# First stage of a banded-attention and gated-product kernel: 256 moving columns read as two halves of 128 in alternation

## The chip, the cores and the metric

The kernel runs on one core of a Trainium2 chip. Its time is the device time in microseconds (us). Before the change the median of three runs is 746.01 us (744.32, 746.01, 748.61). The engines are named as in the profile: PE is TensorE's matmul side, PEld its weight loads, DVE is VectorE, ACT is ScalarE, POOL is GpSimd, SP is SyncE, which issues all DMAs here.

## The reference

Attention over 8 batches and 8 heads, with a band of 32 positions to either side plus 32 global keys, and 32 global queries that see everything, is followed by two products that gate each other and two more products:

```python
x = attn_out.transpose(0, 2, 1, 3).reshape(4352, 512)   # 8 batches x (32 global + 512 local) rows
a = x @ w1                    # w1, w2: 512 x 1024
b = x @ w2
h = (a * b) @ w3              # w3: 1024 x 1024
return h @ w_out              # w_out: 1024 x 512
```

All is float32. Nothing stands between `@ w3` and `@ w_out`, so the kernel multiplies these two weights together once (`fold`, into W34, 1024 x 512) and computes `(a * b) @ W34`.

## The kernel before, in words

The whole program is one static order of steps (the table `ORDER_OF`), interleaved over all engines. What matters here are two stages of TensorE.

**First stage** (`first`, lines 548 to 550 before). The rows of x come in blocks of 256 tokens, 16 blocks of local tokens (`key[0] < B`: batch and half of the batch) and one of the 256 global tokens. For a block, x lies transposed in SBUF: four tiles of 128 features, each `[128, 2, 256]`, with a high part `x[:, 0]` and a low part `x[:, 1]` in the type float32r, which together carry float32. Weights w1 and w2 are split alike into `wh` and `wl`. For each of 8 groups of 128 hidden columns (`m`), for w1 and w2 (`c`, PSUM tiles `ap` and `bp`), and for each of the 4 feature tiles there are three matmuls: wh by high (L548), wh by low (L549), wl by high (L550). The weights, 128 x 128, are the stationary operand and are loaded anew for each matmul (PEld), x's 256 columns are the moving one. That makes 8 x 2 x 4 x 3 = 192 matmuls a block, 3072 over the 16 local blocks and 192 for the global one (tiles `xg`).

**Between the stages**, for two groups `m` at a time: one copy of `ap` to SBUF (`gate_a`, on DVE or ACT), the product with `bp` (`gate_b`, L558, DVE), its high part (`gate_hi`, L442 of a helper) and its low part (`gate_lo`, L445), both float32r tiles `gh` and `gl` of `[128, 2, 256]`. `ap` and `bp` have one buffer each, so the next pair's matmuls wait for `gate_a` and `gate_lo`.

**Second stage** (`second`, L578 to L580). Here gh and gl are stationary, 128 tokens at a time, and a row of 512 columns of W34 is moving; it accumulates in PSUM tiles `acc` of 128 tokens x 512. W34 lies in SBUF with its even columns in front and its odd columns behind them (`by_halves`, `in_pairs`), and the matmul reads it back in order, in alternation from two halves that lie 256 elements apart:

```python
wh, wl = (w.rearrange("p (a c) -> p c a", a=2) for w in W34[m])
```

After 8 groups each `acc` is copied to SBUF (`evict`, L585) and stored (`store`, L593): 128 rows of the output, 2 KB each, 256 KB a DMA, 32 of them for local tokens.

Ahead of and among these stages run the weights' unpacking and folding (L605 to L609, L695 with plain float32 operands), transposes on TensorE (L388), scores (L350, L473) and values (L402, L502) of the attention, as many small matmuls of 32 columns by 64 or 128 rows.

Of the kernel before, what the change touches and what calls it, by code (L numbers as in the profile page):

```python
# [18 lines left out]
def i(ap):  # L19
# [161 lines left out]
    out="D726 A732 D872 D875 A999 A1006 D1109 A1130 A1241 D1254 A1376 D1380 A1519 A1530 D1656 D1666 D1791 D1803  "  # L181
# [20 lines left out]
def band_attention_glu_kernel(  # L202
# [14 lines left out]
    nc = tc.nc  # L217
    B, NP = q_t.shape[0], q_t.shape[1] // 2
    NM, NU = B * NP, B * NP // 2
    TG = 32 * B  # L220
    S = 544
# [317 lines left out]
    def first(key, w, m, c):  # L539

        k_s = f"{key[0]}_{key[1]}_{m - m % 2}"
        if m % 2 == 0:
            T["ab", c] = ps_1.tile([128, 2, 256], F32, tag="ab"[c], name="ab"[c] + "p" + k_s)
        wh, wl = W12[m]
        d = T["ab", c][:, m % 2, 0:w]
        for k in range(4):
            x = X[key[0], k, key[1]]
            nc.tensor.matmul(d, wh[:, k, c, :], x[:, 0, 0:w], start=(k == m % 2 == 0), stop=False, skip_group_check=True)  # L548
            nc.tensor.matmul(d, wh[:, k, c, :], x[:, 1, 0:w], start=False, stop=False, skip_group_check=True)  # L549
            nc.tensor.matmul(d, wl[:, k, c, :], x[:, 0, 0:w], start=False, stop=(k == 3), skip_group_check=True)  # L550

    def gate_a(w, q, eng):
        T["a", q % 2] = p1.tile([128, 2, 256], F32, tag=("as", "g")[q % 2], name="as_")
# [34 lines left out]
    def store(key, w, t):  # L588
        tw = min(w, 128)
        o = T.pop(("o", key, t))  # L590
        if key[0] < B:
            r = key[0] * S + 32 + 256 * key[1] + t
            nc.sync.dma_start(out[r : r + 128], o)  # L593
        else:
            nc.sync.dma_start(out.rearrange("(b s) c -> b s c", s=S)[t // 32 : (t + tw) // 32, 0:32], o[0:tw])

# [274 lines left out]
    def quarter(k, q):  # L871
# [8 lines left out]
        for s, tag in enumerate("ab"):  # L880
            take(tag, 1, (tag, n), ("first", k, m, s))
            for j in range(2):
                me = ("first", k, m + j, s)
                add(me, "PE", ready + made(m + j) + [("first", k, m, s)] * j, first, key, w, m + j, s)
                read(me, (tag, n), *xs)
# [24 lines left out]
        if q == 3:  # L910
            for e in range(0, w, 128):
                me = ("out", k, e)
                take("o", NO, ("o", k, e), me)
                add(me, "ACT DVE", [("second", k, 7, (e,) if last else None)], evict, key, w, e)
                read(me, ("acc", k, e))
                add(("store", k, e), "SP", [me], store, key, w, e)
                read(("store", k, e), ("o", k, e))
# [79 lines left out]
    with tc.manual_schedule(engines=None):  # L997
        for _, n, e in in_order(steps, after):
            fn, args, choice = emit[n]
            k = steps[n][0]  # L1000
# [66 lines left out]
```

## Time and profile before

| what | before |
|---|---|
| median of 3 runs | 746.01 us |
| profiled execution | 744.0 us, its span 742.2 us |
| PE busy | 724.9 us (98%) |
| PEld busy | 645.6 us (87%) |
| DVE / ACT / POOL busy | 429.2 / 292.0 / 115.0 us |
| granted TensorE clock, mean | 0.995 |
| first-stage matmuls on local tokens | 3072 |

Busy time of PE is a poor measure, since matmuls overlap in the pipeline: one of the first stage lasts about 277 ns from its start to its end, while they start some 113 ns apart. The chain of waits shows what each one adds to the end; it gives each matmul the time until the next one starts.

### The profile page before, as it was taken

The page shows a single profiled execution, that of the slowest core. Times are in us where ns is not written, and L with a number is a line of the kernel's source. Part 1 is how long each engine was busy: PE and PEld are TensorE (multiplying, and loading weights), DVE is VectorE, ACT ScalarE, POOL GpSimd, SP SyncE. Part 2 cuts the span into 40 slices and gives each one's busy share as a digit, 9 for nine tenths or more (in the row PEclk, how much of TensorE's full clock was granted, in tenths as well). Part 3 has the DMA queues.
Part 4 walks back from the last instruction along what each step waited for, and adds up shares of the span by engine and source line. Part 5 has one row for each costly group of instructions (what it writes and reads, how often), then busy time and mean ns, then how long its engine had stood idle before and what let it go on. Part 6 is the DMA issues. An engine that isn't in the chain of part 4 may idle for free.

```text
span 742.2 us, 24082 instructions
## 1 busy us (share of the span) xinstructions
PE 724.9 (98%) x10036; PEld 645.6 (87%) x10036; DVE 429.2 (58%) x1275; ACT 292.0 (39%) x853; POOL 115.0 (15%) x165
## 2 busy tenths in 40 slices
PE   4899999999999999999999999999999999999998
PEld 3345598989999998999999999999999999999997
DVE  2788898766565475554765557655566635432232
ACT  3678887654243324324244333244423241301010
POOL 2044565300020002130110001101020110000000
PEclk9899999999999999999999999999999999999999
DMA  8998567797576755577767396756575965520010
GB/s 246 293 303 265 165 216 227 204 265 190 160 214 177 197 152 184 168 191 196 231 174 216 110 243 192 229 137 180 160 216 165 243 169 130 143 72 15 1 43 29
DMA packets 96500, 131.98 MB, mean 178 GB/s; under 512 B 15592, under 2 KB 57704, under 8 KB 96392
## 3 DMA queue, kind: packets, MB, share of 16 engines
q1 hardware_dynamic: 96392, 130.45, 62.1%
q8 instruction: 79, 1.29, 0.7%
q14 instruction: 29, 0.24, 0.1%
HBM read 92.65 MB, written 37.75 MB: 176 GB/s over the span
## 4 chain that ended last, share of the span: by engine, by line
PE 90%; DMA 6%; DVE 1%; POOL 1%; issue 1%; ACT 0%; SPq 0%; DVEq 0%; POOLq 0%
PE ap L548 8%; PE acc L578 8%; PE bp L548 8%; PE ap L549 8%; PE ap L550 8%; PE bp L550 8%; PE bp L549 8%; PE acc L580 8%; PE acc L579 8%; PE w L695 5%; PE v L402 4%; PE s L350 4%; DMA raw_wo<-in_wo_t_dram 3%; PE sg L473 2%; PE gx L502 2%; DMA raw_w12s<-in_w_t_dram 1%
## 5 line engine op out<-in xcount | busy, mean ns | idle before, releaser
L548 PE MATMUL ap<-x,w12h 128*128 128x256 f32 x512 | 143.9, 281 | 0.0
L548 PE MATMUL bp<-x,w12h 128*128 128x256 f32 x512 | 143.8, 281 | 0.0
L549 PE MATMUL ap<-x,w12h 128*128 128x256 f32 x512 | 141.9, 277 | 0.0
L549 PE MATMUL bp<-x,w12h 128*128 128x256 f32 x512 | 141.8, 277 | 0.0
L550 PE MATMUL ap<-x,w12l 128*128 128x256 f32 x512 | 141.8, 277 | 0.0
L550 PE MATMUL bp<-x,w12l 128*128 128x256 f32 x512 | 141.8, 277 | 0.0
L362 ACT ACTIVATE P<-P,mn 128x128 f32<-128x128 f32 x256 | 100.4, 394 | 58.3 <-DVE mn L357 27.1
L548 PEld LDWEIGHTS bp<-x,w12h 128*128 128x128 f32 x512 | 96.3, 188 | 3.3 <-issue 1.6
L548 PEld LDWEIGHTS ap<-x,w12h 128*128 128x128 f32 x512 | 96.3, 188 | 3.2 <-issue 1.8
L549 PEld LDWEIGHTS bp<-x,w12h 128*128 128x128 f32 x512 | 96.2, 188 | 1.4 <-issue 0.2
L549 PEld LDWEIGHTS ap<-x,w12h 128*128 128x128 f32 x512 | 96.2, 188 | 0.9
L550 PEld LDWEIGHTS bp<-x,w12l 128*128 128x128 f32 x512 | 96.2, 188 | 0.0
L550 PEld LDWEIGHTS ap<-x,w12l 128*128 128x128 f32 x512 | 96.1, 188 | 0.0
L357 DVE CUSTOM_DVE_ANT_0 P<-s,cs 128x128 f32<-128x128 f32 x256 | 62.4, 281 | 33.5 <-PE s L350 30.4
L695 PE MATMUL w<-wo,w3f 128*128 128x512 f32 x128 | 61.4, 620 | 4.7 <-DVE w3f L609 4.7
L326 POOL COPY K<-K 128x480 f32<-128x480 f32 x24 | 15.6, 656 | 242.3 <-DMA K<-in_kp_t_dram 204.4
L695 PEld LDWEIGHTS w<-wo,w3f 128*128 128x128 f32 x128 | 23.6, 196 | 30.8 <-issue 22.9
L362 ACT ACTIVATION_READ_ACCUMULATOR P<-P,mn 128x1 f32 x256 | 48.4, 189 | 0.0
L316 POOL COPY V<-vg 32x1024 f32<-32x1024 f32 x26 | 27.0, 1045 | 76.2 <-PE gx L507 44.2
L370 DVE STREAM_TRANSPOSE P<-P 128x1024 f32<-128x1024 f32 x28 | 34.7, 1238 | 5.7 <-ACT P L362 5.6
L316 ACT COPY V<-vg 32x1024 f32<-32x1024 f32 x31 | 32.4, 1045 | 14.0 <-PE gx L507 13.4
L350 PE MATMUL s<-K,q 64*32 64x128 f32 x2048 | 37.6, 277 | 0.0
(786 smaller groups left out, 1362.4 us busy)
## 6 DMA issues: line engine op xcount, KB each, us to landing
Pd<-P SPq DMA_DIRECT2D x112, 128.0 KB, 2.7
Pt<-Pd SPq DMA_DIRECT2D x28, 512.0 KB, 3.9
raw_w<-in_w_t_dram SPq DMA_DIRECT2D x24, 512.0 KB, 5.7
V<-in_v_t_dram SPq DMA_DIRECT2D x56, 192.0 KB, 5.0
K<-in_kp_t_dram SPq DMA_DIRECT2D x36, 272.0 KB, 3.8
V<-in_v_t_dram SPq DMA_DIRECT2D x36, 256.0 KB, 4.9
out_dram<-o SPq DMA_DIRECT2D x34, 256.0 KB, 3.8
q<-in_q_t_dram SPq DMA_DIRECT2D x32, 256.0 KB, 4.5
```

The costliest lines, as they stand in the source:

```text
L316: (nc.scalar.copy if eng is nc.scalar else eng.tensor_copy)(to, src)
L350: nc.tensor.matmul(block(st[:, h], x, 128 * g), q[64 * h : 64 * h + 64, c : c + 32], window(m, h, 4 * g + x), start=True, stop=True, skip_ ...
L357: nc.vector.tensor_tensor_reduce(T["P", m][:, :, h, g], chunks(T["s", m][:, h, 128 * g : 128 * g + 128]), chunks(masks[g]), -0.125, 3.0e38 ...
L362: nc.scalar.activation(P, P, AF.Exp, bias=T["mn", m][:, g, h : h + 1], scale=-1.0, accum_out=T["sm", m][:, g, h : h + 1])
L370: nc.vector.transpose(P, P)
L548: nc.tensor.matmul(d, wh[:, k, c, :], x[:, 0, 0:w], start=(k == m % 2 == 0), stop=False, skip_group_check=True)
L549: nc.tensor.matmul(d, wh[:, k, c, :], x[:, 1, 0:w], start=False, stop=False, skip_group_check=True)
L550: nc.tensor.matmul(d, wl[:, k, c, :], x[:, 0, 0:w], start=False, stop=(k == 3), skip_group_check=True)
L578: nc.tensor.matmul(a, gh[:, m % 2, sl], wh, start=(m == 0), stop=False)
L579: nc.tensor.matmul(a, gh[:, m % 2, sl], wl, start=False, stop=False)
L580: nc.tensor.matmul(a, gl[:, m % 2, sl], wh, start=False, stop=(m == 7))
L695: nc.tensor.matmul(T["w34", t], T["w3f", t, j // 4][:, j % 4], T["wo"][:, j], start=(j == 0), stop=(j == 7))
```

## The change

The moving operand of the first stage is the same 256 columns in another order: column 0 of the block, column 128, 1, 129, and so on (for the global block `a=1`, which leaves the order as it was). The results in `ap`, `bp`, `gh`, `gl` and `acc` then hold the tokens in that order, and the store of 128 rows writes 64 pairs of rows, the two of a pair 128 rows apart. No instruction is added, removed or moved on any engine; after the change the two stage lines are numbered one higher for the first stage (L549 to L551) and the second stage is L579 to L581.

```diff
         for k in range(4):
             x = X[key[0], k, key[1]]
-            nc.tensor.matmul(d, wh[:, k, c, :], x[:, 0, 0:w], start=(k == m % 2 == 0), stop=False, skip_group_check=True)
-            nc.tensor.matmul(d, wh[:, k, c, :], x[:, 1, 0:w], start=False, stop=False, skip_group_check=True)
-            nc.tensor.matmul(d, wl[:, k, c, :], x[:, 0, 0:w], start=False, stop=(k == 3), skip_group_check=True)
+            hi, lo = (x[:, e, 0:w].rearrange("p (a b) -> p b a", a=2 if key[0] < B else 1) for e in range(2))
+            nc.tensor.matmul(d, wh[:, k, c, :], hi, start=(k == m % 2 == 0), stop=False, skip_group_check=True)
+            nc.tensor.matmul(d, wh[:, k, c, :], lo, start=False, stop=False, skip_group_check=True)
+            nc.tensor.matmul(d, wl[:, k, c, :], hi, start=False, stop=(k == 3), skip_group_check=True)
...
         if key[0] < B:
-            r = key[0] * S + 32 + 256 * key[1] + t
-            nc.sync.dma_start(out[r : r + 128], o)
+            r = key[0] * S + 32 + 256 * key[1]
+            to = out[r : r + 256].rearrange("(a b) c -> b a c", a=2)[t // 2 : t // 2 + 64]
+            nc.sync.dma_start(to, o)
```

## Rows read from the trace of the kernel before

**Rows 1.** The page: span, and the granted clock in 40 slices of it.
```profile
span 742.2 us, 24082 instructions
...
PEclk9899999999999999999999999999999999999999
```

**Rows 2.** The page: the chain that ended last, shares of the span by engine.
```profile
PE 90%; DMA 6%; DVE 1%; POOL 1%; issue 1%; ACT 0%; SPq 0%; DVEq 0%; POOLq 0%
```

**Rows 3.** Waits of PE: waiting line, releaser, us in total, times, longest.
```profile
PE w L695 <- DVE w3f L609: 4.7, 1, 4.7
PE v L402 <- DVE raw_w12s L605: 0.2, 1, 0.2
```

**Rows 4.** The page's groups: first stage, output ap (bp alike); busy us, mean ns.
```profile
L548 PE MATMUL ap<-x,w12h 128*128 128x256 f32 x512 | 143.9, 281 | 0.0
...
L549 PE MATMUL ap<-x,w12h 128*128 128x256 f32 x512 | 141.9, 277 | 0.0
```

**Rows 5.** The chain in order of time, first stage: start us, us, what.
```profile
300.20 0.11 PE ap L548
...
302.92 1.03 PE v L402 x64
```

**Rows 6.** The same chain, a run of the second stage.
```profile
313.08 0.22 PE acc L578
...
315.67 0.12 PE bp L548
```

**Rows 7.** Instructions of line 548: duration ns min/median/max, first and last start.
```profile
L548 PE MATMUL ap<-x,w12h x512: 276/276/388, 96.6 to 730.3; 128*128 128x256 f32 x171
```

**Rows 8.** Instructions of line 579, the second stage: one stationary tile.
```profile
L579 PEld LDWEIGHTS acc<-w34l,gh__1203 x4: 188/189/189, 107.4 to 109.4; 128*128 128x128 f32 x4
L579 PE MATMUL acc<-w34l,gh__1203 x4: 379/379/379, 107.7 to 109.6; 128*128 128x512 f32 x4
```

**Rows 9.** Line 548 at 404.2 us: the first matmul after second-stage ones.
```profile
L548 PEld LDWEIGHTS ap<-x,w12h x1: 189/189/189, 404.0 to 404.0; 128*128 128x128 f32 x1
L548 PE MATMUL ap<-x,w12h x1: 286/286/286, 404.2 to 404.2; 128*128 128x256 f32 x1
```

**Rows 10.** Line 578 at 401.5 us: weights loaded while no full matmul streams.
```profile
L578 PEld LDWEIGHTS acc<-w34h,gh__6050 x1: 186/186/186, 401.5 to 401.5; 128*128 128x128 f32 x1
L578 PE MATMUL acc<-w34h,gh__6050 x1: 483/483/483, 401.5 to 401.5; 128*128 128x512 f32 x1
```

**Rows 11.** Timeline at 401.5 us: start us, us, engine, line, operation.
```profile
401.54 0.19 PEld L578 LDWEIGHTS acc<-w34h,gh__6050 128*128 128x128 f32 x1
...
401.65 0.19 PEld L579 LDWEIGHTS acc<-w34l,gh__6050 128*128 128x128 f32 x1
```

**Rows 12.** Line 695, all of it.
```profile
L695 PE MATMUL w<-wo,w3f x128: 592/592/1221, 15.2 to 94.8; 128*128 128x512 f32 x128
```

**Rows 13.** Line 695 at 55.3 us, right behind four transposes.
```profile
L695 PEld LDWEIGHTS w<-wo,w3f x2: 190/191/192, 55.2 to 55.3; 128*128 128x128 f32 x2
L695 PE MATMUL w<-wo,w3f x1: 595/595/595, 55.3 to 55.3; 128*128 128x512 f32 x1
```

**Rows 14.** The chain in order of time: these four transposes.
```profile
54.99 0.44 PE t L388 x4
```

**Rows 15.** Timeline at 640 us: bp's last reader and its next writer.
```profile
639.23 0.65 DVE L445 TENSOR_TENSOR gl__9759<-bp,gh__9757 128x512 fp32r<-128x512 f32 x1
...
640.09 0.30 PE L548 MATMUL bp<-x,w12h 128*128 128x256 f32 x1
```

**Rows 16.** Waits of all engines: DVE for the first stage.
```profile
DVE bp L558 <- PE bp L550: 134.3, 47, 6.2
```

**Rows 17.** Page, DMA issues: KB each, median us to landing.
```profile
Pd<-P SPq DMA_DIRECT2D x112, 128.0 KB, 2.7
...
out_dram<-o SPq DMA_DIRECT2D x34, 256.0 KB, 3.8
```

**Rows 18.** Timeline: the end of the program.
```profile
738.77 0.59 ACT L585 COPY o<-acc 128x512 f32<-128x512 f32 x1 [17.31 <-PE acc L580]
```

## The prediction

> **What bounds the kernel now.** I read the page first, then the chain of waits, then single instructions of the two TensorE stages, to the nanosecond, since the change touches only how long one of 3072 matmuls takes.
>
> The chain says that PE is the bound: 90% of the span lies on it [rows 2], and after the weights are folded (95 us) PE has hardly a wait: its whole list is one of 4.7 us early on, 0.2 us once, and the warm-up's [rows 3]. [...] So a nanosecond off each first-stage matmul comes off the span, as long as no wait replaces it.
>
> A busy time says nothing of a pipelined matmul, so I use two measures. Pace: how far apart starts are. From 300.20 to 302.92 us there are 24 first-stage matmuls [rows 5], 2720 / 24 = 113.3 ns each. From 313.08 to 315.67 there are 12 of the second stage [rows 6], 2590 / 12 = 215.8 ns. Duration: 276 ns at the least and in the median for the first stage [rows 7], 379 for the second [rows 8]. 276 - 113 and 379 - 216 are both 163, so pace = duration - 163, and either can be read for the other.
>
> What is 113.3 made of? [...] 256 columns would be 106.7 + 2.5 = 109.2, a duration of 272. The first stage is 4 ns over this at its best and 5 in the mean: L549 has a mean of 277 [rows 4]. Two causes can make that.
>
> (a) The stream. Right behind a second-stage matmul, a first-stage matmul has had its weights for 100 ns: their load began at 404.0 and took 189, the matmul began at 404.2. Nothing but its own columns can hold it up, and yet it takes 286 [rows 9], 14 over 272. In the second stage, which reads 512 columns in alternation from two halves, there is no such excess: minimum, median and maximum are all 379 [rows 8]. The chip thus reads these float32r columns one behind the other slower than in alternation; beside the weight load the excess varies, and it settles at 4 in long runs.
>
> (b) The weight load. Each first-stage matmul has a load of 128 columns, which can start only when the matmul before begins to stream. Where no full matmul streams, a load takes 186 and its matmul waits 483 - 379 = 104 ns for it [rows 10]; the next load starts 0.11 after the first [rows 11], as soon as that matmul streams. A cycle of load and handing over is thus between 104 and 110; I take 108.5, just below 109.2. But beside a streaming matmul loads take longer: 188 to 189 in the second stage [rows 8], 190 to 192 beside transposes, where the matmul behind them lasts 595 instead of 592 [rows 12, 13], so that it starts to stream 3 ns late. The transposes' pace is 440 / 4 = 110 [rows 14], near 109.2, so they are a fair model; 109.2 + 3 = 112.2.
>
> **The change part by part.** *The moving operand.* 3072 matmuls read in alternation; instruction count, weights and order are the same. The stream should fall from a pace of 114 (277 - 163) to 109.2; the load then decides. Its bounds: 109.2 if loads take no longer than alone, 112.2 if they behave as beside transposes, 113.3 if today's pace is already the load's. The nearest rows are the loads beside an alternating stream, 188.5, 2.5 over the lone load's 186: 108.5 + 2.5 = 111. I take that. 3072 x (114 - 111) = 9.2 us. The 80-odd matmuls that follow the second stage lose about 12 of their 286 as well, 1 us. Together 10 us. The bounds give 3072 x 4.8 + 1 = 16 us and 3072 x 1.8 + 1 = 6.5 us; 113.3 would leave 2 to 3 us. The global block (192 matmuls, a = 1) stays.
>
> [...]
>
> *What could not keep up.* PE pauses for nobody now, so margins matter. The tightest place for bp that I found is at 640 us: its last reader ends at 639.88 and the next writer starts at 640.09 [rows 15], 0.2 us. The matmuls of ap that lie between are 24, and they shrink by 24 x 3 ns = 0.07 us. So it holds. Nor does it add up over the blocks, for DVE itself waits for PE, 134 us in 47 places [rows 16], and moves up with it. I count nothing; if this cover failed at all of the 68 handovers by 0.05 us each, it would cost 3.4 us.
>
> *The stores.* 128 pieces of 2 KB each, as before, but no longer one behind the other in HBM. Only the last one is on the path: its copy starts at 738.77 and takes 0.59, the span ends at 742.2, so 2.8 us are issue and landing [rows 1, 18]. Scattered writes of this kernel land no slower: 2.7 us for 128 KB in small pieces against 3.8 for 256 KB in a row [rows 17]. Bounds: 1 us less to 1 us more; I take 0.
>
> *Other engines* read ap, bp, gh and gl as before, element by element; they do not know the order. 0.
>
> Sum: the profiled execution takes 744.0 us, 742.2 of them the span; -10 makes 734.0. It lies 2.0 under the median of the runs, 746.0, and I forecast that median's successor: 736.0.
>
> **The rivals.**
>
> 1. *The weight load holds the pace at 113.* For it: today's pace of 113.3 [rows 5] is hardly over the 112.2 that loads beside transposes would allow, so stream and load may be equal today. Against it: 286 where no load is waited for [rows 9] shows a slow stream of its own. Then only the disturbed matmuls gain: 0 to 3 us, 743 to 746.
>
> 2. *Alternation collides.* Place: each of the 3072 first-stage matmuls. In the second stage the halves lie 256 elements (1 KB) apart, here 128 (512 bytes), and no row of before reads at that distance. If the two halves, or a half and the weights, hit one place of the memory at once, each matmul pays at least what the worst undisturbed one pays today: 286 - 163 = 123, 9 ns over 114, 28 us in all, 774. It decides where the median duration rises over 277. At the far end, two cycles a column, the pace would be that of the second stage, 216, and the kernel near 746 + 3072 x 0.102 = 1059 us. [...]
>
> 3. *The faster PE runs into others.* DVE's handovers, or loads of keys and values, take half back: 5 us gained, 741. For it: the 0.2 us margins. Against it: DVE's 134 us of waiting for PE [rows 16].
>
> **How the numbers follow.** Forecast (loads near 111, with its bounds 109.2 to 112.2): 0.67, 730 to 741. Rival 1: 0.16, 743 to 747. Rival 2: 0.09. Rival 3: 0.08, 739 to 743. A measurement of this kernel can tell about 0.5%, 3.7 us, from no change, so faster means under 742.3. Faster: all of the forecast, and 0.05 of rival 3: 0.72. Same: rival 1 and the rest of 3, 0.19. Slower: rival 2, 0.09. The range leaves out rival 2 and the edges: 729 to 748; the forecast's own is 730 to 741.
>
> **What the new profile would show.** If right: durations of the three first-stage lines at 274 instead of 276 to 277, with a narrow spread; 24 of them in 2.66 us instead of 2.72; the first one behind the second stage near 273 instead of 286; weight loads at 188 to 189; PE still without waits; the global block unchanged. If loads hold the pace, the first one behind the second stage falls to 273 while the rest stay at 276. If alternation collides, the durations rise over 277. A new row in PE's list of waits would be rival 3. A last store that lands over 4 us after its copy would show that I misjudged the output.

## The result and the profile after

The changed kernel takes 736.65 us (median of 6 runs, 734.39 to 738.30), the kernel before 745.32 (6 runs, the three of above among them): 8.7 us less by the medians. The ratio of the means is 0.9877, with a 95% interval of 0.9850 to 0.9904. The forecast was 736.0, 10 us under a median of 746.0. The profiled execution takes 737.58 us with a span of 735.8, 6.4 less than the span before; so it shows somewhat less than the medians do.

The page after, where it answers to [rows 1, 4]. The first-stage lines are now L549 to L551; the numbers at the end are us busy, then mean ns of one:

```profile
span 735.8 us, 24082 instructions
...
PE 92%; DMA 4%; DVE 1%; ACT 1%; issue 1%; POOL 0%; SPq 0%; DVEq 0%; POOLq 0%; ACTq 0%
...
L549 PE MATMUL ap<-x,w12h 128*128 128x256 f32 x512 | 142.6, 278 | 0.0
...
L550 PE MATMUL ap<-x,w12h 128*128 128x256 f32 x512 | 140.8, 275 | 0.0
```

The mean of the L550 group is 275 where it was 277. All 2048 instructions of L550 and L551 on local tokens take 275, and the first line takes 275 in 914 of 1024 cases: the spread of before (276, 281, 285, 288) has gone.

The chain in order of time, a run of the first stage, as [rows 5]:

```profile
297.51 0.11 PE bp L549
...
301.42 0.11 PE ap L551
301.53 0.47 PE v L402 x24
```

36 matmuls in 4.02 us make 111.7 ns each, where it was 113.3 in a settled run. Over 2932 steps from one such matmul to the next in each trace (all those under 200 ns) the mean goes from 114.4 to 111.6.

Three single matmuls tell why. The first one behind the second stage, as [rows 9], then the one right behind it, and last the first one of the second stage behind the first stage, each with its weight load:

```profile
L549 PEld LDWEIGHTS ap<-x,w12h x1: 189/189/189, 401.5 to 401.5; 128*128 128x128 f32 x1
L549 PE MATMUL ap<-x,w12h x1: 272/272/272, 401.8 to 401.8; 128*128 128x256 f32 x1
```
```profile
L550 PEld LDWEIGHTS ap<-x,w12h x1: 189/189/189, 401.8 to 401.8; 128*128 128x128 f32 x1
L550 PE MATMUL ap<-x,w12h x1: 275/275/275, 401.9 to 401.9; 128*128 128x256 f32 x1
```
```profile
L579 PEld LDWEIGHTS acc<-w34h,gh__5733 x1: 192/192/192, 380.7 to 380.7; 128*128 128x128 f32 x1
L579 PE MATMUL acc<-w34h,gh__5733 x1: 382/382/382, 380.8 to 380.8; 128*128 128x512 f32 x1
```

With its weights there in time, a first-stage matmul takes 272 instead of 286. It is the same in all 77 such places, with 283 to 288 before and 272 or 273 after; the next one starts 109.2 ns behind it in the mean, where it was 121.9. The next one's load ran beside that stream, and already it takes 275 (in all 77 places). A second-stage matmul whose load ran beside the first stage takes 382 (in all 70 such places; before it was 380 in 62 of them) where undisturbed ones take 379: now the load is 3 ns late, and 275 is 272 plus these 3.

PE's waits after, as [rows 3]:

```profile
PE w L697 <- DVE w3f L611: 4.9, 1, 4.9
PE v L402 <- ACT P L362: 0.8, 1, 0.8
PE gx L502 <- DMA Gt<-Gd: 0.8, 1, 0.8
PE v L402 <- issue: 0.7, 1, 0.7
```

Three new ones of 2.3 us in all, at 117, 128 and 154 us, the first two while the weights are still unpacked (until 129 us). The stores land in 3.9 us in the median, 3.8 before [rows 17], and the span ends 3.2 us after the last copy, 2.8 before; that is one execution of each.

### The profile page after: what moved, and what is told of

The parts are those of the page before. It is cut to its first block, busy times and chain, and to the rows that moved or that the text cites. A ratio compares the mean times of both kernels' runs of the same rounds, so it can differ in the third digit from the quotient of the medians.

```text
span 735.8 us, 24082 instructions
## 1 busy us (share of the span) xinstructions
PE 715.6 (97%) x10036; PEld 637.2 (87%) x10036; DVE 432.2 (59%) x1275; ACT 292.3 (40%) x853; POOL 115.1 (16%) x165
## 4 chain that ended last, share of the span: by engine, by line
PE 92%; DMA 4%; DVE 1%; ACT 1%; issue 1%; POOL 0%; SPq 0%; DVEq 0%; POOLq 0%; ACTq 0%
PE ap L549 8%; PE acc L579 8%; PE bp L549 8%; PE bp L551 8%; PE ap L551 8%; PE w L697 8%; PE ap L550 8%; PE bp L550 8%; PE acc L581 8%; PE acc L580 8%; PE s L350 4%; PE v L402 4%; PE sg L473 2%; PE gx L502 2%; DMA raw_wo<-in_wo_t_dram 1%; DMA vg<-in_vg_t_dram 1%
## 5 line engine op out<-in xcount | busy, mean ns | idle before, releaser
L549 PE MATMUL ap<-x,w12h 128*128 128x256 f32 x512 | 142.6, 278 | 0.0
L549 PE MATMUL bp<-x,w12h 128*128 128x256 f32 x512 | 142.4, 278 | 0.0
L550 PE MATMUL bp<-x,w12h 128*128 128x256 f32 x512 | 140.8, 275 | 0.0
L551 PE MATMUL bp<-x,w12l 128*128 128x256 f32 x512 | 140.8, 275 | 0.0
L550 PE MATMUL ap<-x,w12h 128*128 128x256 f32 x512 | 140.8, 275 | 0.0
L551 PE MATMUL ap<-x,w12l 128*128 128x256 f32 x512 | 140.8, 275 | 0.0
L549 PEld LDWEIGHTS bp<-x,w12h 128*128 128x128 f32 x512 | 98.1, 192 | 3.3 <-issue 1.6
L549 PEld LDWEIGHTS ap<-x,w12h 128*128 128x128 f32 x512 | 98.1, 192 | 3.2 <-issue 1.8
L550 PEld LDWEIGHTS bp<-x,w12h 128*128 128x128 f32 x512 | 98.1, 192 | 1.4 <-issue 0.2
L550 PEld LDWEIGHTS ap<-x,w12h 128*128 128x128 f32 x512 | 98.1, 192 | 0.9
L551 PEld LDWEIGHTS bp<-x,w12l 128*128 128x128 f32 x512 | 98.3, 192 | 0.0
L551 PEld LDWEIGHTS ap<-x,w12l 128*128 128x128 f32 x512 | 98.3, 192 | 0.0
L402 PEld LDWEIGHTS v<-V,Pt 128*32 128x32 f32 x2048 | 30.3, 110 | 9.0 <-issue 5.7
```

What stands on the lines that cost most here:

```text
L402: nc.tensor.matmul(vt[32 * x : 32 * x + 32, g, h], t[:, x, h, g], Vs[m % NV][:, x, h, g], start=True, stop=True, skip_group_check=True)
L549: nc.tensor.matmul(d, wh[:, k, c, :], hi, start=(k == m % 2 == 0), stop=False, skip_group_check=True)
L550: nc.tensor.matmul(d, wh[:, k, c, :], lo, start=False, stop=False, skip_group_check=True)
L551: nc.tensor.matmul(d, wl[:, k, c, :], hi, start=False, stop=(k == 3), skip_group_check=True)
```

## The experiments

Theory S: in a row, 256 float32r columns take longer to stream than the 109.2 ns above; in alternation they do not, and then the weight load sets the pace. Its main rivals: the load set the pace before too (L), the alternated stream itself takes 111.6 (A), or the stores gave a part (D).

**The stores alone.** In the changed kernel:

```diff
-            hi, lo = (x[:, e, 0:w].rearrange("p (a b) -> p b a", a=2 if key[0] < B else 1) for e in range(2))
+            hi, lo = (x[:, e, 0:w] for e in range(2))
```

> Only the store of the change; the first stage reads its 256 columns in a row as before (so the rows land in another order). Theory S (the gain is all in the moving read): the time of before within 0.5%, first-stage durations 276 in the median, the first one behind the second stage 285, stores landing in 3.8 us. Rival D (pairs of rows 128 apart change the DMA traffic and give part of the gain): 2 us or more off the time of before.

Measured: 744.84 us against 744.58, ratio 1.0004 (0.9990 to 1.0018); durations as before, while the stores of local tokens land in 3.4 us in the median of this one trace, not in 3.8:

```profile
L550 PE MATMUL bp<-x,w12h x512: 276/276/284, 94.4 to 733.8; 128*128 128x256 f32 x171
```

D, which asked for 2 us or more, falls. Within the 1 us or so that this comparison can tell, all of the gain is in the moving read.

**Half the weights, in alternation and in a row.** The same edit in the changed kernel and in the kernel before:

```diff
+            n = 64 if k else 128
-            nc.tensor.matmul(d, wh[:, k, c, :], hi, ...
+            nc.tensor.matmul(d[0:n], wh[:, k, c, 0:n], hi, ...
```

> The changed kernel, but in the first stage the matmuls of the last three of four feature tiles load only 64 of 128 weight columns (so half the hidden columns lack these features). Theory S (after the change the weight load beside the stream sets the pace of 111.6 ns, the alternated stream itself needs 109.2): matmuls whose weights are half a load start 109.2 ns after the one before, duration 272 to 273, and those with a full load stay at 275. Rival A (alternation at 512 bytes itself streams at 111.6): 275 and 111.6 everywhere.

> The kernel before with the same half loads: 256 columns in a row, three of four feature tiles with 64 weight columns. Theory S (a stream of 256 float32r columns in a row is slower by itself, whatever is loaded): durations stay at 276 or above and the pace at 113 or above, although the load is over 50 ns early. Rival L (the weight load set the pace before the change, and alternation only shortens what load and stream cost each other): 272 to 273 and a pace of 109.2, as with alternation.

In alternation, one of the three lines (min/median/max in ns):

```profile
L551 PEld LDWEIGHTS bp<-x,w12h x512: 136/136/192, 95.8 to 720.7; 128*64 128x64 f32 x128, 128*128 128x128 f32 x43
L551 PE MATMUL bp<-x,w12h x512: 272/273/275, 95.9 to 720.8; 128*64 128x256 f32 x128, 128*128 128x256 f32 x43
```

In a row:

```profile
L550 PEld LDWEIGHTS bp<-x,w12h x512: 133/134/192, 95.7 to 739.2; 128*64 128x64 f32 x128, 128*128 128x128 f32 x43
L550 PE MATMUL bp<-x,w12h x512: 276/277/286, 95.8 to 739.3; 128*64 128x256 f32 x128, 128*128 128x256 f32 x43
```

With loads of 136 ns the alternated stream falls to 273, a pace of 109.2 to 110, and the whole to 732.06 us (one run); of this line's 256 instructions with a full load 255 stay at 275. So the load is what is left of the excess, and A falls. In a row the shorter load frees nothing: 276 at the least, a mean step of 116.0 instead of 114.4, and 750.12 us (one run), slower than before. So L falls too.

One rival is left, that a stream in a row is slow only while another load runs beside it. The same trace settles it: 38 of its matmuls with half a load are the last ones before other work of TensorE, so that the next load starts only some 200 ns after them. One of them, and that next load:

```profile
L551 PEld LDWEIGHTS ap<-x,w12l x1: 134/134/134, 103.6 to 103.6; 128*64 128x64 f32 x1
L551 PE MATMUL ap<-x,w12l x1: 276/276/276, 103.7 to 103.7; 128*64 128x256 f32 x1
```
```profile
103.93 0.27 PEld L350 LDWEIGHTS s<-K,q 64*32 64x32 f32 x21 [0.18 <-issue]
```

All 38 take 276 to 282; the 39 like them in the alternated run take 272 or 273. So reading in a row is slow by itself. Beside full loads more of its matmuls settle at 276 (three in four in the kernel before, half here), and right behind the second stage, with full weights there early, they take 283 to 288. Why a read in a row is slower in these places, where its weights are there sooner, these runs do not tell.

**The distance.** In the changed kernel the tile of x holds half 0 high, half 0 low, half 1 high, half 1 low:

```diff
-            X[key] = p1.tile([128, 2, 256], F32R, tag=tag, ...
+            X[key] = p1.tile([128, 2, 2, 128], F32R, tag=tag, ...
-        hi, lo = (X[key][:, k].rearrange("p (g x q) -> p g x q", g=2, x=4) for k in range(2))
+        hi, lo = (X[key][:, :, k].rearrange("p g (x q) -> p g x q", x=4) for k in range(2))
...
-            hi, lo = (x[:, e, 0:w].rearrange("p (a b) -> p b a", a=2 if key[0] < B else 1) for e in range(2))
+            hi, lo = (x[:, :, e].rearrange("p a b -> p b a") if key[0] < B else x[:, e, 0:w] for e in range(2))
```

> The changed kernel with the tile of x laid out as half 0 high, half 0 low, half 1 high, half 1 low, so that the two halves read in alternation lie 1 KB apart, as in the second stage, instead of 512 bytes. Theory K (the load is slowed by where the stream reads; beside the second stage's alternation at 1 KB it takes 189, here 192): loads at 189, pace 109.2, 3072 x 2.4 = 7 us less than the changed kernel, 729 to 730 against 736.65. Rival N (the distance does not matter; a load beside any stream at full speed takes 192): loads 192, durations 275, the time of the changed kernel within 0.5%, 735 to 738.

```profile
L550 PEld LDWEIGHTS bp<-x,w12h x512: 189/192/192, 96.6 to 729.8; 128*128 128x128 f32 x171
L550 PE MATMUL bp<-x,w12h x512: 275/275/275, 96.7 to 729.9; 128*128 128x256 f32 x171
```

Loads 192 and 275 ns, to the nanosecond as at 512 bytes: K falls, 1 KB and 512 bytes are alike. The time is 738.41 us, just over N's 735 to 738, ratio 0.9926 (0.9906 to 0.9946); the change's interval ends at 0.9904, against other runs of the kernel before, so this layout is at best no faster and may be 0.5% slower. With the same steps in the first stage a difference could only lie elsewhere: its trace is up to 2 us later already when the weights are folded, and waits 1.7 us once where the change waits 0.8. Whether that is the layout stays open.

**Other orders of the same columns.** The stores follow the order (except with runs of four):

```diff
-            hi, lo = (x[:, e, 0:w].rearrange("p (a b) -> p b a", a=2 if key[0] < B else 1) for e in range(2))
+            hi, lo = (x[:, e, 0:w].rearrange("p (a b) -> p b a", a=128 if key[0] < B else 1) for e in range(2))
```

with 128, 64, 16 and 4 for `a`, and with `"p (a b c) -> p b a c", a=2, c=4` for the runs of four.

> The changed kernel with 128 parts of 2 columns in place of 2 parts of 128: the even columns of a block in order, then the odd ones, neighbours in the stream 8 bytes apart, two of them in each 16 bytes. Theory P (far places must alternate): as slow as in a row, durations 276 and more, 285 behind the second stage. Rival Q (columns in the same 16 bytes right behind each other are slow): somewhat slow, above 275. Rival R (only the very next address is slow): 275 as in the changed kernel, 273 behind the second stage.

> The changed kernel with 64 parts of 4 columns: columns 0, 4, 8 and so on, then 1, 5, 9: neighbours in the stream 16 bytes apart. Theory P (far places must alternate): as slow as in a row, 276 and more, 285 behind the second stage. Rivals Q and R (16 bytes shared, or the next address, is what is slow): 275, and 273 behind the second stage.

> The changed kernel, but four columns in a row from one half, then four from the other: 16 bytes here, 16 bytes there (the rows of a block land in another order). Theory P (far places must alternate, by 16 bytes is enough): 275, and 273 behind the second stage. Rivals Q and R (columns of one 16 bytes, or neighbours, right behind each other are slow): three of four steps are slow, 276 and more, 285 behind the second stage.

> The changed kernel with 4 parts of 64 columns read in turn, neighbours in the stream 256 bytes apart, each place four times in 16 bytes before it moves on. Theory F (few places taken in turn are kept open, so that 16 bytes are fetched once): 275, and 273 behind the second stage, as with two parts. Rival E (each step to other 16 bytes costs, as at 8 and 16 bytes distance, and two parts are the exception): over 390 and near 1100 us.

> The changed kernel with 16 parts of 16 columns read in turn, neighbours in the stream 64 bytes apart. Theory F (only few places are kept open; 16 are too many): as slow as 64 parts, over 390 and near 1100 us. Rival G (the distance decides, and 64 bytes are enough): 275, as with two parts.

The same line in each, first 128 parts, then 64, 16, 4, and the runs of four:

```profile
L550 PE MATMUL bp<-x,w12h x512: 407/425/429, 96.2 to 1087.5; 128*128 128x256 f32 x171
```
```profile
L550 PE MATMUL bp<-x,w12h x512: 412/415/433, 95.0 to 1096.4; 128*128 128x256 f32 x171
```
```profile
L550 PE MATMUL bp<-x,w12h x512: 396/400/415, 96.4 to 1057.3; 128*128 128x256 f32 x171
```
```profile
L550 PE MATMUL bp<-x,w12h x512: 302/308/315, 97.2 to 820.6; 128*128 128x256 f32 x171
```
```profile
L550 PE MATMUL bp<-x,w12h x512: 286/290/299, 95.3 to 771.5; 128*128 128x256 f32 x171
```

| order | neighbours in the stream | median ns | mean step, ns | us (one run) |
|---|---|---|---|---|
| two halves in turn (the change) | 512 bytes | 275 | 111.6 | 736.65 (median of 6) |
| in a row (before) | 4 bytes | 276 | 114.4 | 745.32 (median of 6) |
| four from one half, four from the other | 4, or 512 bytes | 290 | 126.8 | 782.70 |
| 4 parts in turn | 256 bytes | 308 | 142.4 | 831.88 |
| 16 parts | 64 bytes | 400 | 220.3 | 1070.56 |
| 64 parts | 16 bytes | 415 | 233.4 | 1117.24 |
| 128 parts | 8 bytes | 425 | 229.7 | 1098.56 |

The step is the distance from one first-stage start to the next (those over 1.5 times the median are left out). It goes with the time; for the slow orders the duration less 163 is more than the step.

None of the theories that I had written down fits all of it. Far places as such are not what helps (P fails with the runs of four, Q and R with 64 parts), and "few places are kept open" (F) fits 16 parts but should have made 4 parts free; E and G fail with 4 and with 16 parts. Two places in turn, one column each, is the one order here that streams without excess; what in the memory makes it so stays open. Where single columns are taken in turn, the number of places and the distance between neighbours changed together in these runs. Two places nearer to each other, or four that lie 512 bytes apart, were not tried, so which of the two decides is open as well.

**Taking the new waits away, and the global block too.** In the changed kernel the two values and the product of global queries for which PE waits move a few places back in the order, and the global block is read in alternation, with two stores of 64 rows in place of one of 128:

```diff
-    v="190 278 339 394 541 597 693 761 ...
+    v="190 278 339 394 541 611 693 772 ...
...
-    vg="644 770 ...
+    vg="654 770 ...
...
-            hi, lo = (x[:, e, 0:w].rearrange("p (a b) -> p b a", a=2 if key[0] < B else 1) for e in range(2))
+            hi, lo = (x[:, e, 0:w].rearrange("p (a b) -> p b a", a=2) for e in range(2))
```

> The changed kernel with two more edits: the values of two pairs of heads and one product of global queries, for which TensorE waited 2.3 us at 117, 128 and 154 us in the changed kernel's profile, are put one or two pieces of work later in TensorE's order, and the global block is read in alternation too, with its stores to match. Theory W (TensorE has other work for that time, and the global block gains as the others did): those three waits gone, global durations 280 to 275, together 2.3 + 192 x 6.3 ns = 3.5 us under the changed kernel, a ratio to before of 0.983. Rival V (the waits are the pace of the transposed weights' way through HBM and come back behind): other waits of 1 to 2 us in their place, a ratio of 0.986 to 0.988.

```profile
PE sg L473 <- DVE mn L357: 0.5, 1, 0.5
PE ap L549 <- DVE w12h L442: 0.2, 1, 0.2
PE ap L551 <- DVE w12l L445: 0.2, 1, 0.2
```
```profile
L550 PE MATMUL ap<-xg,w12h x32: 275/275/275, 663.9 to 690.1; 128*128 128x256 f32 x32
```

The global block does gain (280 to 275), and the three waits are gone, but others of 0.9 us stand behind them, and the matmuls behind this stretch start only 0.6 us earlier than in the changed kernel's trace. The time is 737.69 us, ratio 0.9901 (0.9878 to 0.9924): its interval overlaps that of the change, so no gain is shown. W holds for the global block; for the waits V is nearer in this one trace, since most of the time came back.

## Why the prediction was right

*The bound.* PE's chain held: the steps between matmuls gave 8.5 us, and the medians lie 8.7 apart. With half loads in alternation the first stage's steps gave 13.0 us, and the last matmul starts 12.3 us earlier than before.

*(a) The stream.* Right, and shown apart from the load: 286 to 272 where the weights are early, and the half loads leave reading in a row at 276 or more. My number for the first was 273. Its weights were early, by about the 100 ns that I had named: in all 77 places the load ends 24 or 25 ns before the matmul's start, while before the change 2436 of the 2963 loads behind another first-stage matmul of a local block end 77 or 78 ns behind it. I had written that nothing but its own columns could hold that matmul up; a load for the next one runs beside it, and only the 38 matmuls with half loads and none beside them rule it out.

*(b) The load sets what is left.* Right in kind, and near in size partly by luck. I took a load of 188 to 189 beside the stream and a pace of 111, durations of 274. Measured are a pace of 111.6 and 275; the loads take 189 where one first runs beside the alternated stream, and 192 in the runs behind it. My sum starts from 108.5 for a lone load's cycle, which I picked between 104 and 110 and which no run measures. With loads of 189 it gives 108.5 + 3 = 111.5; with 192 it would give 114.5, no gain at all. The matmul that a load of 189 feeds already lasts 275, so the 189 is nearer to what counts, but that 108.5 was the right start is not shown. The model of the transposes [rows 13], in which the stream begins 3 ns late, gives 112.2 and needs no such pick. The running matmul lost nothing to the load beside it here: 272 or 273 with a full load of 189 there, in the 77 places, and 272 or 273 with none, in the 39 of the half-load run. The load itself takes 186 alone and 189 to 192 here. Why it takes longer, no run here separates. That a load waits for the matmul before it, the trace of before shows: of 4026 such loads within the two stages, 3868 start 2 to 4 ns after that matmul's start and none sooner.

*The sum.* The trace of before does not show the 106.7 + 2.5 from which I had 109.2 and 272. The trace after has steps of 109.2 in the 77 places and of 216 in the median in the second stage, so that 256 columns more take 106.8 and 2.4 are left. I had 9.2 us of steps and 1 us for the entries behind the second stage. Added up over the two traces, the 2963 steps from one first-stage matmul of a local block to the next, the entries among them, got shorter by 8.3 us, and the 70 steps from there into the second stage by 0.2: 8.5 instead of 10.2, for the pace of 111.6 instead of 111. The forecast of 736.0 came within 0.7 us of the median partly by luck: it took 10 us off 746.0, while the gain was 8.7 and the six runs of before have a median of 745.3.

*What could not keep up.* Here I counted nothing and forecast PE without waits; the profiled execution has three new ones of 2.3 us. I had looked for margins between the two stages, which did hold; the waits lie in a stretch of attention that I had not looked at. One is for `Gt`, which comes back through HBM; of the two at the values (L402) the profile puts one down to ACT and names nothing for the other, so that the way of their inputs through HBM holds them up is a guess. The starts of PE's instructions show what this execution lost: at 160 us the changed kernel is 0.15 us behind the kernel before although the first stage has saved 1.15 by then; from there on the first stage gains 7.3 us, other steps lose 0.4, and the last matmul starts 6.8 us earlier.

That the faster first stage causes these waits is not shown. Each kernel has one trace, and PE's waits differ among them. First the stores alone, then half loads in a row, then half loads in alternation:

```profile
PE bp L551 <- issue: 0.5, 1, 0.5
PE gx L502 <- DMA Gt<-Gd: 0.4, 1, 0.4
PE v L402 <- DMA Pt<-Pd: 0.2, 1, 0.2
```
```profile
PE v L402 <- issue: 0.7, 1, 0.7
PE s L350 <- DMA q<-in_q_t_dram: 0.6, 1, 0.6
```
```profile
PE v L402 <- ACT P L362: 0.4, 1, 0.4
PE bp L550 <- DVE gl__1980 L445: 0.3, 1, 0.3
```

The first two read in a row and yet wait at the three places where the changed kernel does (0.2, 0.4 and 0.7 us there); the third has the fastest first stage of all and waits 0.7 us in total. And the steps gave 8.5 us; less 2.3 that would be 6.2, while the measured gain is 8.7 by the medians and, by the interval of the ratio, at least 7.2. This speaks against 2.3 us lost in a usual execution.

*The stores.* 0, as counted: ratio 1.0004 with the stores alone.

*The rivals.* The first (the load holds 113) fell: a settled run went from 113.3 to 111.7, and with half loads a read in a row stays at 113 and more. The second (alternation collides) did not come about at 512 bytes, but it was no idle fear: with 64 parts the mean step is 233, over the second stage's 216 [rows 6] that I had put at the far end, and the kernel at 1117 us, past the 1059 that I had worked out from it. My 0.09 for it was an estimate. For the third rival there are the three waits of one trace, which may not be the change's; the medians do not show it.

## What to carry to other kernels

Judge a stream of matmuls by one whose weights were early: if another order of the same columns makes it shorter (286 in a row here, 272 in alternation), the read is slow. By how much, a settled run tells better: in a row it was 285 in the one case and 276 in the other. Where 256 float32r columns are moving, an order that takes one column from each of two halves in turn is worth a trial; four parts put the starts 31 ns further apart here than two, 16 and more over 100. And before calling a new wait in one trace the change's own, look for it in the traces of kernels that lack the change.

## What I had not expected of the hardware

- Shorter loads made reading in a row slower: a mean step of 116.0 with three quarters of the loads halved, 114.4 with full ones.
- Runs of four columns (16 bytes) from two halves in turn are slower than a row: 290 against 276.
- Loads beside a slow stream take longer too: about 208 with 128 parts, 192 in the change, 186 alone.
